# First loads on two DMA queues, folds and K behind the first V tiles, and store waits spread over the queue

## The chip, the cores and the metric

The kernel runs on one core of a Trainium2 chip. A core has a matrix engine (PE, TensorE), three engines for elementwise work (DVE, VectorE; ACT, ScalarE; POOL, GpSimd), a queue engine (SP, SyncE), and 16 DMA engines that move data between the chip's memory and the core's own memory. SP and ACT can both issue DMAs, each on a queue of its own. The metric is device time in microseconds. The median before is 277.26 us over 4 runs (277.1 to 277.8).

## The reference

The kernel computes one transformer block in bf16 on 2048 tokens of width 640: a linear attention with 32 heads of width 20 and a gated MLP with 1536 columns, both fed by the same layer norm, in parallel, plus the input.

```python
def _A_ref(x, wqkv, w_phi, wo):
    qkv = (x @ wqkv).reshape(B, S, 3, H, Dh)           # to q, k, v per head
    pq = einsum("bhsd,hdf->bhsf", q, w_phi)
    pk = einsum("bhsd,hdf->bhsf", k, w_phi)
    phi_q = concatenate([softmax(pq), softmax(-pq)])
    phi_k = concatenate([softmax(pk), softmax(-pk)])
    kv = einsum("bhsf,bhsd->bhfd", phi_k, v)
    z  = einsum("bhsf->bhf", phi_k)
    num = einsum("bhqf,bhfd->bhqd", phi_q, kv)
    den = einsum("bhqf,bhf->bhq", phi_q, z)[..., None] + 1e-6
    return (num / den).reshape(B, S, D) @ wo

def _B_ref(x, w1, w3, w2):
    return (silu(x @ w1) * (x @ w3)) @ w2

xn = _layernorm(x)
return x + _A_ref(xn, ...) + _B_ref(xn, ...)
```

## The kernel before

The 2048 tokens are 16 tiles of 128 (T), or 4 blocks of 512 (NB). The width 640 is 5 chunks of 128 (DC), the MLP's 1536 columns are 12 chunks (FC). The names of the work on PE, in the order in which it first appears:

- **cT** (xc_transpose, L726): the first four tiles of x, with their mean taken off but not yet scaled, are transposed on PE. centre (L719) takes off the mean: ACT sums the tile (an activation with an accumulator, from which z = -mean comes), and DVE or ACT adds z.
- **V** (v_first, L744, for tiles 0 to 3; v_tile, L829, for the others): 10 matmuls of 320 columns against wv. v_first uses the transposes of the centred tile and scales by 1/std when the result leaves PSUM, so it need not wait for the normalised tile.
- **xT** (xn_transpose, L758): the normalised tiles 0 to 3 are transposed on PE into xnT. Tiles 4 to 15 are transposed by DMA (turn, L628).
- **fold** (L783): wk (later wq) is multiplied by w_phi, so that the feature map's first matmul disappears. It needs wqkT, the transposed weights, which five DMA transposes bring (load_wT, L652), and BDc, a block diagonal form of w_phi which POOL builds (block_diag, L774). The result is copied to Wkp.
- **K** (k_tile, L838): 10 matmuls of 320 columns against Wkp, then two Exps on ACT. k_norm (L846) sums on DVE and divides on POOL.
- **MLP columns** (mlp, L955): 10 matmuls of 512 columns, a tanh on ACT, two products on DVE. One column covers 128 of the 1536 and one block of tokens, 512, so the first block's columns need xnT of tiles 0 to 3.
- later: kv_sum, kv_back, q_proj, q_tok (attention's second half) and out_tile (L973), which multiplies by w2 and wo, adds x and stores.

ln_stats (L697) computes mean and variance on DVE and 1/std on POOL; ln_apply (L712) normalises a tile, on DVE for tiles 0 to 3, on DVE or ACT for the later ones.

The order of the instructions is not written by hand. Each operation is recorded with a level (its priority, partly a due time through when) and the engines that could do it, each with a duration. schedule (L168) then plays the kernel in a model: at each step it takes the earliest operation, and between operations that are about equally early the one with the highest level. Constants of the model are MODE (the switch of PE between tile shapes), BACKLOG (how far DMA issues may run ahead of the modelled bus) and the bytes per second of the bus (330e3 bytes per us in commit). The early attribute keeps an operation from being planned before a given time, and filler puts matmuls on zeros into PE's early gaps. The program is fixed when it is built: emit (L384) writes the list of each engine, with a semaphore wait where an operation needs another engine's result, and every engine works through its own list in order. At the end of SP's list stands a wait for every store of the output (L434).

All DMAs are issued by SP. In the order of its list: x tiles 0, 1 and 2; wv in five pieces of one chunk; x tile 3; w_phi; the first 256 columns of w1 and of w3; the five transposes of wk; x tiles 4 to 7; and then the rest of w1 and w3 with x tiles 8 to 11 and 12 to 15 between them; the transposes of xnT as tiles become ready, with those of wq between them.

A single helper records each kind of instruction, so matmuls carry L559, elementwise work L567, plain DMAs L626 and DMA transposes L632; the names of the tiles tell them apart.

Of the kernel before, what the change touches and what calls it, by code (L numbers as in the profile page):

```python
# [2 lines left out]

ACT = mybir.ActivationFunctionType
ALU = mybir.AluOpType
# [4 lines left out]
D = 640  # L10
# [9 lines left out]

ENGINES = ("PE", "ACT", "DVE", "POOL", "SP")
SEM = {"PE": 0.06, "ACT": 0.04, "DVE": 0.04, "POOL": 0.08, "SP": 0.05}
MODE = 0.097
GRAN = 8
BACKLOG = 2.5


def heads_of_chunk(c):
# [37 lines left out]
class _Program:  # L66
# [98 lines left out]

    def schedule(self, start, filler=None, filler_until=0.0):  # L168
        for n, o in enumerate(self.all):
            o.idx = n  # L170
            o.war -= o.raw
# [42 lines left out]
        def commit(o, e, t):  # L214
            nonlocal bus, pool_prev
            o.eng = e
            o.emit, o.busy, dur = o.ways[e]
            o.start = t
            free[e] = t + o.busy
            if o.nbytes:  # L220
                bus = max(bus, t + 0.6) + o.nbytes / 330e3
                o.end = bus + 1.2 + o.extra
            else:
                o.end = t + dur
            o.done = True
# [66 lines left out]
        while left:  # L292
            best = None
            pick = None
            if ready_u:
                t0 = free["PE"]
                blocked = set()
                cands = []
                for u in ready_u:
                    extra = MODE if u.mode != mode else 0.0  # L300
                    u.at = max(unit_time(u), t0 + extra)
                for u in sorted(ready_u, key=lambda u: (-u.level, u.mms[0].idx)):
                    opts = []
                    for k in range(0, 8, u.banks):
                        if blocked & set(range(k, k + u.banks)):
                            continue
                        g = group_time(u, k)
                        if g < 1e8:
                            opts.append((max(g, u.at), fit(k, u.banks, u.at), k))
                    if opts:  # L310
                        x = min(opts)
                        if pick is None or x[0] < pick[0] - (0.03 + MODE):
                            pick = (x[0], u, x[2])
                    if u.banks == 4 and u.at <= t0 + 1.0 and not blocked and (not opts or x[0] > u.at + 0.03):
                        k = min((group_time(u, k, True), k) for k in (0, 4))[1]
                        blocked |= set(range(k, k + 4))
                if pick is not None:
                    best = (pick[0], "PE", pick[1], pick[2])
            moved = False
            for e in ("ACT", "DVE", "POOL", "SP"):  # L320
                if not ready[e]:
                    continue
                ts = [(max(free[e], op_time(o, e)), o) for o in ready[e]]
                t = min(x[0] for x in ts)
                t, o = min((x for x in ts if x[0] <= t + 0.09), key=lambda x: (-x[1].level, x[1].idx))
                if len(o.ways) > 1 and o.level > 1.5e6:
                    other = min(max(free[f], op_time(o, f)) + o.ways[f][2] for f in o.ways if f != e)
                    if other < t + o.ways[e][2] - 0.02:
                        ready[e].remove(o)
                        del o.ways[e]  # L330
                        moved = True
                        continue
                if best is None or t < best[0]:
                    best = (t, e, o, None)
# [49 lines left out]
    def emit(self, finish):  # L384
        nc = self.nc
        for n, o in enumerate(self.ops):
            o.idx = n
        for o in self.ops:
# [22 lines left out]
        for o in self.ops:  # L411
            k = know[o.eng]
            for d in sorted(o.deps, key=lambda d: -d.idx):
# [4 lines left out]
                for a, b in d.clock.items():  # L418
                    if k.get(a, 0) < b:
                        k[a] = b  # L420
                k[key[0]] = max(k.get(key[0], 0), key[1])
            if o.nbytes:
                ndma += 1
                s = nc.alloc_semaphore(f"d{ndma}")
# [6 lines left out]
            else:  # L431
                lists[o.eng].append(("op", o.emit, None, 0))
            o.clock = dict(k)
        for o in finish:  # L434
            lists["SP"].append(("wait", o.sem[2], o.sem[1]))
        return lists
TRIPLES = ((0, 3, 0, 60), (3, 3, 60, 60), (6, 3, 120, 60), (9, 3, 180, 60), (12, 3, 240, 60), (13, 3, 300, 20))


def bass_parallel_sum__linear_kernel_hedgehog__glu_gated_swiglu__prompt_kernel(  # L440
# [134 lines left out]
    def sb(*aps):  # L575
        return [a for a in aps if hasattr(a, "ap")]
# [42 lines left out]

    queue = {"SP": nc.sync, "ACT": nc.scalar}  # L620

    def load(o, i, level=0.0, eng="SP", after=()):
        n = mybir.dt.size(o.dtype)
        for s in o.shape:
            n *= s
        return P.dma(eng, lambda: queue[eng].dma_start(o, i), sb(o), sb(i), n, 0.45, level, after)  # L626

    def turn(o, i, level=0.0, dram=False):  # L628
        n = 2
        for s in o.shape:  # L630
            n *= s
        d = P.dma("SP", lambda: nc.sync.dma_start_transpose(o, i), sb(o), sb(i), n, 1.3 * n / 163840, level)  # L632
        d.extra = 1.0 if dram else 0.2
        return d

# [9 lines left out]
    def load_x(a, b, level, eng="SP"):  # L645
        load(x_tok[:, a:b, :], x_t[:, a:b, :], level, eng)

    def load_w13(a, b, level):
        load(w1_s[:, :, a:b], w1_t[:, :, a:b], level)
        load(w3_s[:, :, a:b], w3_t[:, :, a:b], level)  # L650

    def load_wT(which, e, level):  # L652
        turn(wqkT[:, which * DC + e:which * DC + e + 1, :],
# [6 lines left out]
    def consts():  # L660
        memset("DVE", zero[:], 0.0, 9)
        zeroed.append(P.all[-1])
        memset("DVE", warm[:], 0.0, 9)
        add([w_act(warm[:], warm[:], ACT.Exp, 8)], [warm[:]], [warm[:]], None, 1e9)
# [47 lines left out]
    def ln_apply(t, level):  # L712
        o, m, s, z = x_tok[:, t, :], mv[:, t, 0:1], mv[:, t, 4:5], mv[:, t, 6:7]
        ways = [w_op("DVE", "tensor_scalar", (o, o, m, s, ALU.subtract, ALU.mult), 0.35, 0.44)]
        if t >= 4:
            ways.append(w_act(o, o, ACT.Identity, D, s, z))
        add(ways, [o], [o, m, s, z] if t >= 4 else [o, m, s], None, level)

    def centre(t, level):  # L719
        o, i, z = xc[:, t, :], x_tok[:, t, :], mv[:, t, 6:7]  # L720
        add([way("ACT", "activation", (junk[:], i, ACT.Copy), dict(scale=-1.0 / D, accum_out=z), 0.8, 0.9)],
            [junk[:], z], [i], None, level)
        add([w_op("DVE", "tensor_scalar", (o, i, z, None, ALU.add), 0.35, 0.44), w_act(o, i, ACT.Identity, D, 1.0, z)],
            [o], [i, z], None, level)

    def xc_transpose(t, level):  # L726
        n = 2 if t == 0 else 1
# [287 lines left out]
    lv = 9e5  # L1015
    load_x(0, 1, lv)
    load_x(1, 2, lv - 1)
    load_x(2, 3, lv - 2)
    for c in range(DC):
        load(wv[:, c, :], wqkv_t[:, c, 2 * D:3 * D], lv - 3 - c)  # L1020
    load_x(3, 4, lv - 8)
    load(phi_s[:], phi_t, lv - 9)
    load_w13(0, 256, lv - 10)
    for e in range(DC):
        load_wT(1, e, lv - 12 - e)
    load_x(4, 8, lv - 19)
    load_w13(256, 512, lv - 20)
    load_x(8, 12, lv - 21)
    load_w13(512, 1024, lv - 22)
# [10 lines left out]
    block_diag(0)  # L1040
    late(n, 8.0)
    for t in range(4):
        centre(t, up - t)
        ln_apply(t, 1e5 - t)
    for t in range(4):
        xc_transpose(t, 6e4 - 10 * t + 15)
    for t in range(4):
        xn_transpose(t, 3e4 - t)
    for t in range(4, T, 2):
        ln_stats(t, 2, 1e5 - t)  # L1050
        ln_apply(t, 2e5 - t)
# [5 lines left out]
        return 1000.0 - us  # L1057

    for t in range(4):
        v_first(t, 6e4 - 10 * t)  # L1060
    for dc in range(DC):
        fold(1, dc, 4e4 - dc)
    for t in range(T):
# [29 lines left out]
    for t in range(T):  # L1093
        out_tile(t, when(200 + 5 * t))

    P.schedule({"PE": 1.25, "ACT": 2.1, "DVE": 0.93, "POOL": 0.8, "SP": 0.81}, filler, 12.0)

    lists = P.emit(finish)

# [58 lines left out]
```

## Time and profile before

| | us |
|---|---|
| median of 4 runs | 277.26 |
| the profiled execution | 277.1 |
| its span (first to last instruction) | 275.3 |
| PE busy | 269.3 |
| DVE, ACT, POOL busy | 183.3, 102.0, 60.6 |

A profile shows one execution. For each engine it gives the time in which instructions ran, and the idle time before an instruction with what ended it. The chain that ended last goes back from the last instruction: at each step to what released it, or to the instruction before it on its engine. A DMA's issue is an instruction on the queue; the transfer itself takes longer and ends with a landing. "SPq" is SP's queue, "PEld" the loading of weights into PE, which overlaps with matmuls. Matmuls are pipelined: one of 320 columns is shown with 299 ns, but ten of them start within 1.36 us.

### The profile page before, as it was taken

To read this page: it belongs to the slowest core of one execution; us is meant where nothing else is said; L and a number is where in the kernel's file an instruction comes from. 1 tells how busy PE (TensorE), PEld (TensorE's weight loads), DVE (VectorE), ACT (ScalarE), POOL (GpSimd) and SP (SyncE) were. 2 spreads that over 40 slices of the span, in tenths; PEclk is the share of its full clock that TensorE was granted. 3 is DMA by queue.
4 is the path that set the end of the run, shared out by engine and by line. 5 is a ranking of instruction groups with operands and counts; after the bars stand their busy time and mean duration, and the time that the engine had idled before them with its cause. 6 is when DMAs were issued, how large, how long until landed. Compare 5 with 4: busy or idle time off the path is not lost.

```text
span 275.3 us, 5058 instructions
## 1 busy us (share of the span) xinstructions
PE 269.3 (98%) x2094; PEld 159.1 (58%) x2094; DVE 183.3 (67%) x324; ACT 102.0 (37%) x188; POOL 60.6 (22%) x101
## 2 busy tenths in 40 slices
PE   8999899999999999999999999999999999999996
PEld 4656576656654447544444445677777774444774
DVE  5769789999987443578978979577761215666112
ACT  6555768455454441246673472010000002322000
POOL 3601664999799100000000000000000000000000
PEclk9999999999999999999999999999999999999999
DMA  6989996840000000801211141243342222000001
GB/s 190 212 232 353 282 147 120 140 147 2 0 0 2 0 0 2 280 9 26 48 26 24 27 47 24 74 100 95 97 97 71 74 71 71 2 0 0 26 24 48
DMA packets 41303, 21.98 MB, mean 80 GB/s; under 512 B 27072, under 2 KB 41280, under 8 KB 41280
## 3 DMA queue, kind: packets, MB, share of 16 engines
q1 hardware_dynamic: 41280, 21.66, 31.8%
q8 instruction: 16, 0.26, 0.4%
q14 instruction: 7, 0.06, 0.1%
HBM read 12.81 MB, written 2.62 MB: 56 GB/s over the span
## 4 chain that ended last, share of the span: by engine, by line
PE 84%; SPq 5%; DMA 4%; DVE 3%; ACT 2%; issue 1%; POOL 0%
PE PS L559 84%; SPq L632 3%; DMA xnT<-x_tok 2%; SPq L626 2%; DMA x_tok<-in_A_x_dram 2%; ACT EqT L567 2%; DVE bst L567 1%; POOL mv L567 0%; DVE hT L567 0%; DVE t L567 0%; DVE Wkp L567 0%; DVE den_s L567 0%; DVE xres L567 0%; DVE x_tok L567 0%; DVE mv L567 0%
## 5 line engine op out<-in xcount | busy, mean ns | idle before, releaser
L559 PE MATMUL PS<-xnT,w_s 128*128 128x512 bf16 x480 | 108.6, 379 | 0.9 <-DVE xnT L567 0.6
L559 PEld LDWEIGHTS PS<-xnT,w_s 128*128 128x128 bf16 x480 | 46.1, 98 | 54.5 <-DVE hT L567 0.8
L559 PE MATMUL PS<-w_s,hT 128*128 128x320 bf16 x384 | 55.0, 299 | 0.0
L567 ACT ACTIVATE th<-PS 128x512 f32<-128x512 f32 x48 | 28.8, 599 | 65.1 <-PE PS L559 65.1
L567 DVE SCALAR_TENSOR_TENSOR t<-th,PS 128x512 bf16<-128x512 f32 x48 | 32.9, 684 | 25.4 <-ACT th L567 25.4
L559 PEld LDWEIGHTS PS<-w_s,hT 128*128 128x128 bf16 x384 | 37.1, 98 | 14.9
L567 DVE TENSOR_TENSOR xres<-PS,xres 128x640 bf16<-128x640 f32 (+1 forms) x17 | 13.3, 785 | 41.2 <-PE PS L559 41.2
L567 POOL TENSOR_TENSOR ekt<-ekt,rS 128x640 bf16<-128x640 bf16 x32 | 39.5, 1270 | 4.5 <-DVE rS L567 4.4
L567 DVE SCALAR_TENSOR_TENSOR hT<-t,PS 128x512 bf16<-128x512 bf16 x48 | 32.4, 676 | 1.4 <-PE PS L559 0.3
L567 ACT ACTIVATE EqT<-PS 128x512 bf16<-128x512 f32 x40 | 21.9, 595 | 12.6 <-PE PS L559 12.6
L567 ACT ACTIVATE ekt<-PS 128x640 bf16<-128x640 f32 x32 | 20.8, 701 | 10.4 <-PE PS L559 10.2
L559 PE MATMUL PS<-wo_s,oT 128*128 128x320 bf16 x160 | 24.5, 299 | 0.0
L567 DVE TENSOR_TENSOR prod<-PS,g_s 128x1280 bf16<-128x1280 f32 x16 | 23.8, 1490 | 0.5
L567 DVE TENSOR_REDUCE S<-ekt 128x64 f32<-128x1280 bf16 x16 | 22.9, 1458 | 1.6 <-ACT ekt L567 1.6
L559 PE MATMUL PS<-Wkp,xnT 128*128 128x320 bf16 x160 | 23.9, 299 | 0.0
L559 PE MATMUL PS<-xnT,Wqp 128*128 128x512 bf16 x100 | 23.6, 380 | 0.0
L567 ACT ACTIVATE e_s<-PS 128x64 f32<-128x64 f32 x32 | 9.1, 283 | 37.6 <-PE PS L559 37.1
L559 PE MATMUL PS<-wv,xnT 128*128 128x320 bf16 x120 | 18.3, 299 | 1.0 <-DMA xnT<-x_tok 1.0
L559 PEld LDWEIGHTS PS<-wo_s,oT 128*128 128x128 bf16 x160 | 15.7, 98 | 6.1
L559 PEld LDWEIGHTS PS<-Wkp,xnT 128*128 128x128 bf16 x160 | 15.6, 98 | 6.1
L559 PEld LDWEIGHTS PS<-wv,xnT 128*128 128x128 bf16 x120 | 11.7, 98 | 7.0 <-issue 1.4
L559 PEld LDWEIGHTS PS<-xnT,Wqp 128*128 128x128 bf16 x100 | 9.3, 98 | 10.8
(69 smaller groups left out, 170.8 us busy)
## 6 DMA issues: line engine op xcount, KB each, us to landing
w_s<-in_B_w_dram SPq DMA_DIRECT2D x4, 640.0 KB, 9.0
xres<-in_A_x_dram SPq DMA_DIRECT2D x16, 160.0 KB, 2.3
out_dram<-xres SPq DMA_DIRECT2D x15, 160.0 KB, 1.8
x_tok<-in_A_x_dram SPq DMA_DIRECT2D x3, 640.0 KB, 8.1
w_s<-in_B_w_dram SPq DMA_DIRECT2D x1, 1920.0 KB, 9.1
w_s<-in_B_w_dram SPq DMA_DIRECT2D x4, 320.0 KB, 5.7
wv<-in_A_wqkv_dram SPq DMA_DIRECT2D x5, 160.0 KB, 4.0
wo_s<-in_A_wo_dram SPq DMA_DIRECT2D x1, 800.0 KB, 5.7
```

What stands on the lines that cost most here:

```text
L559: return nc.tensor.matmul(o(u.k), l, r, start=start, stop=stop, skip_group_check=shared)
L567: return getattr(e, name)(*[at(a, u) for a in args], **{k: at(v, u) for k, v in kw.items()})
L626: return P.dma(eng, lambda: queue[eng].dma_start(o, i), sb(o), sb(i), n, 0.45, level, after)
L632: d = P.dma("SP", lambda: nc.sync.dma_start_transpose(o, i), sb(o), sb(i), n, 1.3 * n / 163840, level)
```

## The change

It has these parts.

1. **The first loads.** SP issues x tiles 0 and 1, chunks 0 and 1 of wv as one piece, x tiles 2 and 3, then the five wk transposes, and only then w1 and w3. ACT issues chunks 2 to 4 of wv as one piece and w_phi, directly behind the activation that warms up its table, and later, behind the evacuation of the first V tile, x tiles 4 to 7.
2. **Centring.** The constant CENTRED says which engine centres which of the first four tiles. Tiles 0 and 1 keep the sum on ACT; for tiles 2 and 3 DVE subtracts the mean of the statistics.
3. **Normalising on POOL.** ln_apply of tiles 0 and 1 runs on POOL instead of DVE.
4. **The order on PE.** With the new levels, durations and constants the planner arrives at this: V0 and V1 one behind the other; cT2, xT0, xT1, cT3; V2 and V3; xT2 and xT3; all five folds; K of tiles 0 to 3; five MLP columns; then V4, K4 and so on up to K9 before the next column. Before, it was: V0, cT2, V1, cT3, V2, V3; all four xT; a column; three folds; a column; two folds; a column; K of tiles 0 to 3; a column; then V4 up to K8.
5. **Planner.** The bus is modelled in time per descriptor size instead of bytes; MODE goes from 0.097 to 0.085 and BACKLOG from 2.5 to 5.0; within the first 25 us of the model the planner's tolerances are drawn at random from a fixed seed.
6. **Store waits.** Before the n-th output store SP waits for store n - 4, and at its end only for the last four.

The further order, up to the last instruction, differs in a few places: the wq transposes stand at other places between the xnT transposes, POOL's last divisions change places with two memsets, and one MLP column changes places with two projections of q in the attention's second half.

```diff
-MODE = 0.097
+MODE = 0.085
-BACKLOG = 2.5
+BACKLOG = 5.0
...
+        rng = random.Random(seed)
...
-                bus = max(bus, t + 0.6) + o.nbytes / 330e3
+                bus = max(bus, t + 0.6) + o.nbytes / 1e3
...
+                slack = 0.12 if seed is None or t0 > shaken else rng.choice((0.03, 0.12, 0.12, 0.3, 0.6))
...
-                        if pick is None or x[0] < pick[0] - (0.03 + MODE):
+                        if pick is None or x[0] < pick[0] - slack:
...
+            if o in place and place[o] >= 4:
+                d = finish[place[o] - 4]
+                lists[o.eng].append(("wait", d.sem[2], d.sem[1]))
...
-        for o in finish:
+        for o in finish[-4:]:
             lists["SP"].append(("wait", o.sem[2], o.sem[1]))
...
+CENTRED = {0: "ACT", 1: "ACT", 2: "DVE", 3: "DVE"}
+POOLED = (0, 1)
+SEED = 0
...
+    def bus(o, elem):
+        n = 1
         for s in o.shape:
             n *= s
+        return n * 2 / elem / 16 * max(18.0, 10 + 0.0352 * elem) + 100.0
...
+        if t in POOLED:
+            ways = [w_op("POOL", "tensor_scalar", (o, o, m, s, ALU.subtract, ALU.mult), 1.25, 1.3)]
...
+    def centre(t, level, by):
+        if by == "ACT":
...
+        else:
+            m = mv[:, t, 0:1]
+            add([w_op("DVE", "tensor_scalar", (o, i, m, None, ALU.subtract), 0.35, 0.44)], [o], [i, m], None, level)
...
     load_x(1, 2, lv - 1)
-    load_x(2, 3, lv - 2)
-    for c in range(DC):
-        load(wv[:, c, :], wqkv_t[:, c, 2 * D:3 * D], lv - 3 - c)
-    load_x(3, 4, lv - 8)
-    load(phi_s[:], phi_t, lv - 9)
-    load_w13(0, 256, lv - 10)
+
+    def load_wv(a, b, level, eng):
+        load(wv[:, a:b, :], wqkv_t[:, a:b, 2 * D:3 * D], level, eng)
+    load_wv(0, 2, lv - 2, "SP")
+    load_x(2, 3, lv - 3)
+    load_wv(2, 5, 2e9, "ACT")
+    load_x(3, 4, lv - 4)
+    load(phi_s[:], phi_t, 2e9 - 1e3, "ACT")
     for e in range(DC):
-        load_wT(1, e, lv - 12 - e)
-    load_x(4, 8, lv - 19)
+        load_wT(1, e, lv - 9 - e)
+    load_w13(0, 256, lv - 16)
+    n = len(P.all)
+    load_x(4, 8, 1.9e6, "ACT")
+    late(n, 9.0)
...
     for t in range(4):
-        xc_transpose(t, 6e4 - 10 * t + 15)
-    for t in range(4):
-        xn_transpose(t, 3e4 - t)
+        if t in CENTRED:
+            xc_transpose(t, 6e4 - 10 * t + 15)
+        xn_transpose(t, 3e4 - t if t in CENTRED else 6e4 - 10 * t + 15)
...
-    P.schedule({"PE": 1.25, "ACT": 2.1, "DVE": 0.93, "POOL": 0.8, "SP": 0.81}, filler, 12.0)
+    P.schedule({"PE": 1.25, "ACT": 2.1, "DVE": 0.93, "POOL": 0.8, "SP": 0.81}, filler, 12.0, SEED, 25.0)
```

More of the change, by code (lines that the diff above doesn't have):

```diff
@@ L2 @@
 from concourse import mybir
+import random
 ACT = mybir.ActivationFunctionType
@@ L164, in dma, with schedule @@
         return self.add(o, writes, reads, level, after)
-    def schedule(self, start, filler=None, filler_until=0.0):
+    def schedule(self, start, filler=None, filler_until=0.0, seed=None, shaken=0.0):
+        rng = random.Random(seed)
         for n, o in enumerate(self.all):
@@ L324, in schedule @@
                 t = min(x[0] for x in ts)
-                t, o = min((x for x in ts if x[0] <= t + 0.09), key=lambda x: (-x[1].level, x[1].idx))
+                w = 0.09 if seed is None or t > shaken else rng.choice((0.03, 0.09, 0.09, 0.2, 0.4))
+                t, o = min((x for x in ts if x[0] <= t + w), key=lambda x: (-x[1].level, x[1].idx))
                 if len(o.ways) > 1 and o.level > 1.5e6:
@@ L387, in emit @@
             o.idx = n
+        finish = sorted(finish, key=lambda o: o.idx)
+        place = {o: n for n, o in enumerate(finish)}
         for o in self.ops:
@@ L620, in bass_parallel_sum__linear_kernel_hedgehog__glu_gated_swiglu__prompt_kernel, with load @@
     queue = {"SP": nc.sync, "ACT": nc.scalar}
-    def load(o, i, level=0.0, eng="SP", after=()):
-        n = mybir.dt.size(o.dtype)
+    def bus(o, elem):
+        n = 1
         for s in o.shape:
             n *= s
-        return P.dma(eng, lambda: queue[eng].dma_start(o, i), sb(o), sb(i), n, 0.45, level, after)
+        return n * 2 / elem / 16 * max(18.0, 10 + 0.0352 * elem) + 100.0
+    def load(o, i, level=0.0, eng="SP", after=()):
+        return P.dma(eng, lambda: queue[eng].dma_start(o, i), sb(o), sb(i), bus(o, 2 * o.shape[-1]), 0.45, level,
+                     after)
     def turn(o, i, level=0.0, dram=False):
[L629 to L632, printed above, removed]
+        d = P.dma("SP", lambda: nc.sync.dma_start_transpose(o, i), sb(o), sb(i), bus(o, 256),
+                  1.31, level)
         d.extra = 1.0 if dram else 0.2
@@ L646, in load_x, with load_w13 @@
         load(x_tok[:, a:b, :], x_t[:, a:b, :], level, eng)
-    def load_w13(a, b, level):
-        load(w1_s[:, :, a:b], w1_t[:, :, a:b], level)
-        load(w3_s[:, :, a:b], w3_t[:, :, a:b], level)
+    def load_w13(a, b, level, eng="SP"):
+        load(w1_s[:, :, a:b], w1_t[:, :, a:b], level, eng)
+        load(w3_s[:, :, a:b], w3_t[:, :, a:b], level, eng)
     def load_wT(which, e, level):
@@ L663, in consts @@
         memset("DVE", warm[:], 0.0, 9)
-        add([w_act(warm[:], warm[:], ACT.Exp, 8)], [warm[:]], [warm[:]], None, 1e9)
+        add([w_act(warm[:], warm[:], ACT.Exp, 8)], [warm[:]], [warm[:]], None, 3e9)
         memset("POOL", ident[:], 0.0)
@@ L717, in ln_apply @@
         add(ways, [o], [o, m, s, z] if t >= 4 else [o, m, s], None, level)
-    def centre(t, level):
+    def centre(t, level, by):
         o, i, z = xc[:, t, :], x_tok[:, t, :], mv[:, t, 6:7]
[L721 to L724, printed above, removed]
+        if by == "ACT":
+            add([way("ACT", "activation", (junk[:], i, ACT.Copy), dict(scale=-1.0 / D, accum_out=z), 0.86, 0.92)],
+                [junk[:], z], [i], None, level)
+            add([w_op("DVE", "tensor_scalar", (o, i, z, None, ALU.add), 0.35, 0.44),
+                 w_act(o, i, ACT.Identity, D, 1.0, z)], [o], [i, z], None, level)
+        else:
+            m = mv[:, t, 0:1]
+            add([w_op("DVE", "tensor_scalar", (o, i, m, None, ALU.subtract), 0.35, 0.44)], [o], [i, m], None, level)
     def xc_transpose(t, level):
@@ L1042, in bass_parallel_sum__linear_kernel_hedgehog__glu_gated_swiglu__prompt_kernel @@
     for t in range(4):
-        centre(t, up - t)
+        if t in CENTRED:
+            centre(t, up - t, CENTRED[t])
         ln_apply(t, 1e5 - t)
     for t in range(4):
-        xc_transpose(t, 6e4 - 10 * t + 15)
-    for t in range(4):
-        xn_transpose(t, 3e4 - t)
+        if t in CENTRED:
+            xc_transpose(t, 6e4 - 10 * t + 15)
+        xn_transpose(t, 3e4 - t if t in CENTRED else 6e4 - 10 * t + 15)
     for t in range(4, T, 2):
@@ L1059, in bass_parallel_sum__linear_kernel_hedgehog__glu_gated_swiglu__prompt_kernel @@
     for t in range(4):
-        v_first(t, 6e4 - 10 * t)
+        (v_first if t in CENTRED else v_tile)(t, 6e4 - 10 * t)
     for dc in range(DC):
```

## The prediction

> **What bounds the kernel now.** I read the page's busy shares and the chain that ended last first, then the chain in order of time, then the timelines of PE and of SP's queue over the first 35 us.
>
> ```profile
> PE 269.3 (98%) x2094; PEld 159.1 (58%) x2094; DVE 183.3 (67%) x324; ACT 102.0 (37%) x188; POOL 60.6 (22%) x101
> ```
> ```profile
> 14.25 5.22 DMA x_tok<-in_A_x_dram
> ...
> 26.08 5.96 DMA xnT<-x_tok
> 32.05 0.14 issue
> 32.18 102.14 PE PS L559 x825
> ...
> 144.53 128.21 PE PS L559 x984
> 272.73 0.02 issue
> 272.76 0.49 DVE xres L567
> ```
>
> PE is busy 98% of the span, and from 32.18 us on the chain is nearly all matmul: 102.14, then a seam of some 10 us, then 128.21. The same multiplications have to be done afterwards, so nothing but empty time on PE can be won. Between 40 and 272 us PE has only 0.3 us of it. The rest is before 32.18 us, where the chain is SP's queue, a load of x, statistics and a DMA transpose. PE's own timeline there (start, length, work, idle before it):
>
> ```profile
> 6.34 2.26 PE L559 MATMUL PS<-wv,xcT 128*128 128x320 bf16 x10
> 8.44 0.44 PE L736 MATMUL PS<-ident,xc 128*128 128x128 bf16 x5
> 8.72 1.52 PE L559 MATMUL PS<-wv,xcT 128*128 128x320 bf16 x10
> ...
> 15.33 2.33 PE L559 MATMUL PS<-xnT,w_s 128*128 128x512 bf16 x10 [0.59 <-DVE xnT L567]
> 17.50 1.11 PE L559 MATMUL PS<-BDc,wqkT 128*128 128x140 bf16 x18
> ...
> 28.90 2.32 PE L559 MATMUL PS<-xnT,w_s 128*128 128x512 bf16 x10
> 32.18 1.52 PE L559 MATMUL PS<-wv,xnT 128*128 128x320 bf16 x10 [0.96 <-DMA xnT<-x_tok]
> ```
>
> "Busy" up to 6.3 us is mostly filler. The prizes are the late start of V0 at 6.34 (it waits for wv, chunk by chunk), 0.59 us before the first MLP column, and 0.96 us before V4, which waits for a DMA transpose. SP's queue explains the last one:
>
> ```profile
> 2.19 2.33 SPq L626 DMA_DIRECT2D wv<-in_A_wqkv_dram  x5
> ...
> 7.03 7.18 SPq L632 DMA_TRANSPOSE wqkT<-in_A_wqkv_dram  x5
> 14.25 0.58 SPq L626 DMA_DIRECT2D x_tok<-in_A_x_dram  x1
> ```
>
> x tiles 4 to 7 are issued only behind five wk transposes (1.27 us each, the first 1.93), at 14.25; they land at 19.48, and everything up to V4 hangs on that.
>
> **Step 1, first loads.** Issues cost 0.43 us each, one per 0.47. Before, x0, x1, x2, wv in five pieces and x3 go one behind another. PE's first five pairs of V0 start at 6.2, 6.8, 7.2, 7.7 and 8.15 us as the pieces land, x3 lands at 8.9. In the change SP has x0, x1, two chunks of wv, x2, x3; ACT has the other three chunks and then phi. ACT issues them behind its table load (0.80 to 2.08) and the warming Exp (to 2.30), so at 2.3 and 2.8.
> Does the second queue bring wv sooner? V0's last matmul needs wv, x0 and x1; what shares the bus with it decides. Before, x0 to x2 and wv are 8 x 164 = 1,311 KB. After, if two queues share equally from 3.2 us, ACT's 492 KB finish when SP has also moved 492 KB (its wv piece and x2), behind 328 KB of x0 and x1: 1,312 KB, the same. The windows of 2:4 and 6:8 us show the DMA engines at a share of 0.91 and 1.03 while moving 266 and 285 GB/s. The Trainium skill's page "DMA: Bandwidth & Descriptors" (Issuing engines are not separate DMA queues) speaks against a gain: all queues end on the same 16 engines, and a second one only saves issue time. The row speaks a little the other way: landings 0.48 us apart match the issue rhythm of 0.475, and between 20 and 25 us the same engines move 349 GB/s. By the rule wv is complete at 8.15 as before; by the row, 1,311 KB from 2.0 us at 330 GB/s plus the 1.25 us that now lie between moving and landing, at 7.2. I take 8.15, because shares of 0.9 to 1.0 are a busy bus; 7.2 is the good end, and 8.9 (ACT's part served last, with x3) the bad end.
> What is late next: x2, which landed by 4.95, now lands with wv's end at about 8.15, x3 at 8.8.
>
> **Step 2, V0 to the last transpose.** V0's last six matmuls after 8.15: 0.8, to 8.97; V1 1.36 (ten starts, 0.136 each), to 10.33. Before, PE had V1 done at 10.24 and the transpose of tile 2 as well, so here the change is behind by 0.4.
> DVE is in order: second half of the statistics of x1, first half of x2 (waits for x2), and only behind it tile 1's aggregate. So from 8.2: 0.44, aggregate 0.2 (8.85), x2 to 9.5, x3 first half 9.95, centring tile 2 10.35 (0.39), x3 second half and aggregate 11.0, centring tile 3 11.4, copy of xcT2 11.9 (0.47). ACT loses two centring passes (2 x 0.92); the two DVE centrings stand where they did.
> POOL now normalises tiles 0 and 1. The trace has no POOL operation of that form; nearest is its 128x640 multiply at 1.27 us (two inputs), the lower end is the 0.22 of the 128x1 form. I take 1.27. Tile 1's rstd starts at 8.9, ends 9.7; tile 2's first half 9.95; the normalising of tile 1 to 11.2; then tile 2's and 3's rstd among five BDc products (4 x 0.42 + 0.58), done about 14.9. Before, BDc was done at 11.5 and waited.
> PE then: cT2 at 10.4, xT0, xT1 to 11.5, cT3 to 11.75, V2 from 12.0 (xcT2's copy), V3 to 14.7, xT2 and xT3 to 15.25. Without DVE's lateness it would be 14.85. So the folds start at 15.25, where the old kernel started its first column at 15.33: the front as such wins 0.1.
>
> **Step 3, folds and K directly, columns after.** Before, columns lay between folds to cover the five Wkp copies (ACT 0.67, DVE 0.82). Now: folds 0.95 + 0.68 = 1.63, to 16.9; ACT copies three (15.75 to 17.75, behind V3's evacuation), DVE two (behind two xnT copies, 16.2 to 17.75). K0 needs its bank and chunk 1 at 17.0, chunks 3 and 4 at 17.8, and reaches those 0.8 us after its start. So K starts at 17.05, a loss of 0.2; bounds 0 and 0.8 (K0 standing for all five copies). wk transposes, issued from 3.15 to 10.2 now, land by about 14 (3.0 to 5.3 us after issue). K takes 5.44 (23.46 to 28.90), eight Exps of 0.67 keep its pace.
> Then five columns instead of four before V4: 5 x 2.165 = 10.8. V4 at 17.05 + 5.44 + 10.8 + 0.1 = 33.4.
>
> **Step 4, does V4 still wait?** ACT issues x4 to x7 behind V0's evacuation, at about 10.0 instead of 14.25; its issue was 0.58, and V1's evacuation is queued behind it, with slack. It lands at about 15.2. DVE reaches those statistics after the Wkp copies, at 17.8, normalises at 22. SP issues the transposes at about 22.5 behind all but one of the w1/w3 loads; 5.2 MB left at 10.2 us and 340 GB/s are moved at 25.7, so they land at 27 to 29. V4 at 33.4 has 4 us of cover; without it, 0.96 again. The weights of columns 1 to 4 land by 17, those of the fifth by 24 and it starts at 31. After V4, tiles 8 and 9 come behind one more wq transpose (1.3 us); they are needed at 44. No stall.
>
> **Step 5, store waits.** Before, 17 waits stand at SP's end. But the queue's waits show that it still stood there for the last store:
>
> ```profile
> SPq L1103 <- DMA out_dram<-xres: 0.8, 1, 0.8
> ```
>
> The 13 waits removed are hidden by that 0.8; without it they cost some 0.5 us. Each added one waits for the store four back, landed long ago (1.8 us each, 5 us apart): zero to 0.05, on the last store. Behind them stand only that store and a residual load with slack. New planner constants and seed change only orders; late ones swap a column and two q projections at 155 to 167 us, same work: 0, bounds -0.3 to +0.3 from the seam's own 0.3.
>
> **Sum.** Old V4 with a fifth column ahead: 32.18 + 2.16 = 34.34. New: 33.4. Gain 0.95. The profiled execution took 277.1 with a span of 275.3 and 1.8 around it: it becomes 274.35 and 276.15. The median lies 0.16 above that: **276.3**.
>
> **Rivals.** *Main line* (gain 0.5 to 1.6, 275.7 to 276.7): chance 0.50.
> *The second queue speeds the bus* (for: 349 GB/s later; against: the share already at 0.9): wv at 7.2 and x2 early move folds from 15.25 to some 14.3: 275.3 (275.0 to 275.7). Chance 0.15.
> *The change doesn't do what it says*: wv at 8.9 puts the folds 0.5 to 0.7 later, or the copies stall K by 0.8: 276.7 to 277.8. For: two queues, x3 and transposes compete with wv. Against: equal sharing. Chance 0.17.
> *Slower: PE's clock stays low.* The page's clock row says 9 throughout, but five transposes take 0.74 us at 5.81 and 0.44 at 8.44, and the first V0 matmul 474 ns against 299. So PE reached full speed near 6.9 us, after 5.6 us without a break. The Trainium skill's page "TensorE: Matmul & The Clock Gate" (What's actually happening) says that the clock is raised after a window of some 3.4 us of sustained work. In the change PE idles from 6.3 to 7.1 and again before 8.15. By the row alone the switch comes at 6.9 as before; by the rule a window that covers the idle may fail. Then V0's last six and V1's ten matmuls take 0.267 instead of 0.136: +2.1, 278.4. It decides from the eighth slow matmul on (0.95 / 0.131). Against: the window before 6.3 is as full as now. With it, 0.18.
>
> **Range and chances.** 275.0 (the quick bus) to 278.4 (the slow clock); the likeliest case alone 275.7 to 276.7. A measurement here tells 0.2%, 0.55 us. Faster: 0.50 + 0.15 + 0.02 = 0.67; within: 0.12 of the third case; slower: 0.18 + 0.03 = 0.21.
>
> **What would show it.** wv's last chunk at 8.15 and V0 ending at 9.0; folds starting at 15.25 with BDc done before; K with no gap above 0.3; V4 at about 33.4 with no DMA ahead of it; the tail's wait longer than 0.8. It is wrong if V0 ends after 9.8, if matmuls of 474 ns go on beyond 8 us, if V4 or V5 waits for a transpose, or if PE's idle time moves behind 40 us.

## The result, and the profile after

The median after the change is 276.61 us (276.3 to 277.04, 41 runs); beside it the kernel before took 277.13 us (276.49 to 277.98, 61 runs). The ratio is 0.9979, 95% interval [0.9974, 0.9984]: a gain of 0.58 us by the ratio (0.52 between the medians), where 0.95 was forecast. The profiled span went from 275.3 to 274.9 us.

The busy shares of the kernel after are nearly those of before; POOL alone has 5 us more:

```profile
PE 269.0 (98%) x2097; PEld 159.7 (58%) x2097; DVE 183.0 (67%) x319; ACT 102.6 (37%) x187; POOL 65.6 (24%) x103
```

The chain that ended last, in order of time (start, length, what):

```profile
4.89 0.78 POOL mv L580
5.67 0.10 issue
5.77 2.53 POOL x_tok L580
8.30 0.22 POOL mv L580
8.52 0.07 issue
8.59 0.79 POOL mv L580 x2
9.38 0.01 issue
9.39 2.54 POOL x_tok L580
11.93 0.05 issue
11.98 0.45 PE PS L787 x5
...
15.99 117.77 PE PS L572 x935
```

Before, the chain was SP's queue, a load of x, its statistics and a DMA transpose as far as 32.18 us, and only from there PE. Now PE carries it from 11.98 us on (but for a seam of some 10 us in the middle that both kernels have), and what stands ahead of that is POOL: two normalisings (x_tok, L580) of 2.53 us each, with the 1/std of tile 1 (mv) between them. The prediction had 1.27 us for each of these.

PE's timeline (start, length, work, idle before it) shows the same place from the other side:

```profile
6.92 2.88 PE L572 MATMUL PS<-wv,xcT 128*128 128x320 bf16 x20
...
9.91 0.44 PE L787 MATMUL PS<-ident,x_tok 128*128 128x128 bf16 x5
...
11.98 0.45 PE L787 MATMUL PS<-ident,x_tok 128*128 128x128 bf16 x5 [1.63 <-POOL x_tok L580]
...
12.55 2.88 PE L572 MATMUL PS<-wv,xcT 128*128 128x320 bf16 x20
15.27 0.72 PE L787 MATMUL PS<-ident,x_tok 128*128 128x128 bf16 x10
15.83 1.76 PE L572 MATMUL PS<-BDc,wqkT 128*128 128x140 bf16 x30
17.54 5.61 PE L572 MATMUL PS<-Wkp,xnT 128*128 128x320 bf16 x40
22.98 10.96 PE L572 MATMUL PS<-xnT,w_s 128*128 128x512 bf16 x50
33.77 1.52 PE L572 MATMUL PS<-wv,xnT 128*128 128x320 bf16 x10
```

V0 and V1 now run without a break from 6.92 to 9.63 us, the second of two sets of xT waits 1.63 us for POOL, and from 12 us to V4 nothing waits: V4 starts at 33.77 with no DMA ahead of it. The old kernel with a fifth column before V4 would stand at 34.34, so the front has won 0.57 us. The last DVE operation starts at 272.27 instead of 272.76, 0.49 earlier: the gain is made before V4, and the rest of the kernel passes it on.

Up to the folds the change is still behind: they start at 15.83, where the old kernel's first column stood at 15.33, 0.50 earlier. The gain is V4's wait of 0.96, which is gone, less these 0.50, and 0.11 that is made up between the folds and V4.

ACT's queue, and SP's, show the loads (start, length of the issue, transfer):

```profile
1.26 0.45 ACTq L642 DMA_DIRECT2D wv<-in_A_wqkv_dram  x1
1.74 0.51 ACTq L642 DMA_DIRECT2D phi_s<-in_A_w_phi_dram  x1
...
8.48 0.38 ACTq L642 DMA_DIRECT2D x_tok<-in_A_x_dram  x1
```
```profile
3.30 6.96 SPq L646 DMA_TRANSPOSE wqkT<-in_A_wqkv_dram  x5
...
22.48 7.91 SPq L646 DMA_TRANSPOSE xnT<-x_tok  x4
```

ACT issues wv at 1.26 us, within its table load (0.81 to 2.09) and ahead of the warming Exp that stands before it in ACT's list (2.10); the prediction had 2.3.

### The profile page after: what moved, and what is told of

Read it like the earlier page. It is cut to its first block, busy times and chain, and to the rows that moved or that the text cites. A ratio compares the mean times of both kernels' runs of the same rounds, so it can differ in the third digit from the quotient of the medians.

```text
span 274.9 us, 5072 instructions
## 1 busy us (share of the span) xinstructions
PE 269.0 (98%) x2097; PEld 159.7 (58%) x2097; DVE 183.0 (67%) x319; ACT 102.6 (37%) x187; POOL 65.6 (24%) x103
## 4 chain that ended last, share of the span: by engine, by line
PE 92%; POOL 3%; ACT 2%; DVE 1%; DMA 1%; issue 1%
PE PS L572 91%; POOL x_tok L580 2%; ACT EqT L580 2%; DMA x_tok<-in_A_x_dram 1%; POOL mv L580 1%; PE PS L787 0%; DVE bst L580 0%; DVE hT L580 0%; DVE den_s L580 0%; DVE xres L580 0%; ACT e_s L580 0%; DVE xc L580 0%; PE PS L757 0%; DVE t L580 0%; DVE pr_s L580 0%
## 5 line engine op out<-in xcount | busy, mean ns | idle before, releaser
L580 ACT ACTIVATE th<-PS 128x512 f32<-128x512 f32 x48 | 28.8, 599 | 66.1 <-PE PS L572 66.1
L580 DVE SCALAR_TENSOR_TENSOR t<-th,PS 128x512 bf16<-128x512 f32 x48 | 32.6, 678 | 24.0 <-ACT th L580 24.0
L580 DVE TENSOR_TENSOR xres<-PS,xres 128x640 bf16<-128x640 f32 (+1 forms) x17 | 13.3, 785 | 41.2 <-PE PS L572 41.2
L580 POOL TENSOR_TENSOR ekt<-ekt,rS 128x640 bf16<-128x640 bf16 x32 | 39.5, 1264 | 1.6 <-DVE rS L580 1.6
L580 DVE SCALAR_TENSOR_TENSOR hT<-t,PS 128x512 bf16<-128x512 bf16 x48 | 32.5, 677 | 1.3 <-PE PS L572 0.3
L580 ACT ACTIVATE EqT<-PS 128x512 bf16<-128x512 f32 x40 | 21.9, 594 | 12.6 <-PE PS L572 12.6
L580 DVE TENSOR_REDUCE S<-ekt 128x64 f32<-128x1280 bf16 x16 | 22.9, 1459 | 3.4 <-ACT ekt L580 3.4
L580 DVE TENSOR_TENSOR prod<-PS,g_s 128x1280 bf16<-128x1280 f32 x16 | 23.8, 1490 | 0.5
L580 ACT ACTIVATE ekt<-PS 128x640 bf16<-128x640 f32 x32 | 20.8, 701 | 8.6 <-PE PS L572 8.4
L580 ACT ACTIVATE e_s<-PS 128x64 f32<-128x64 f32 x32 | 9.0, 282 | 37.6 <-PE PS L572 37.1
L580 DVE BATCH_NORM_STATS2 bst<-x_tok 128x6 f32<-128x320 bf16 x32 | 14.2, 468 | 3.1 <-DMA x_tok<-in_A_x_dram 3.1
L572 PEld LDWEIGHTS PS<-xnT,Wqp 128*128 128x128 bf16 x100 | 9.3, 98 | 10.8
```

Of the source, the lines that this page charges most:

```text
L572: return nc.tensor.matmul(o(u.k), l, r, start=start, stop=stop, skip_group_check=shared)
L580: return getattr(e, name)(*[at(a, u) for a in args], **{k: at(v, u) for k, v in kw.items()})
```

## The experiments

Three questions were open: what POOL's normalising costs and why; what of the earlier wv is due to the second queue; and which of the other parts (early x tiles 4 to 7, store waits, filler and clock) carry time. All start from the kernel after and keep its planned order on every engine, except where a new plan is named.

**Both tiles normalised on DVE.**

```diff
...
+    for t in (0, 1):
+        a, (e, (f, busy, dur)) = applied[t]
+        a.eng, a.emit = e, f
...
```

`applied` holds each normalising and the same operation for DVE.

> The changed kernel with its order kept, only the normalising of tiles 0 and 1 runs on DVE instead of POOL. Theory A (POOL's two normalisings of 2.53 us each are what ate the front's gain): PE's wait of 1.6 us before the transpose of tile 1 is gone, V2 starts at about 11.4 instead of 12.55, folds at about 14.7 instead of 15.83, time 1.1 us below the changed kernel: about 275.5, ratio to before 0.994. Theory B (DVE is in order and full, so the wait only moves to the centring of tile 3, to BDc or to the copies): V2 not before 12.2, time 276.3 to 276.8, ratio 0.997 to 0.999.

Measured: 275.12 us (274.92 to 275.57) against 277.11 of before, ratio 0.9933 [0.992, 0.9947]. This beats both kernels. Its PE timeline:

```profile
6.67 2.88 PE L572 MATMUL PS<-wv,xcT 128*128 128x320 bf16 x20 [0.41 <-DMA wv<-in_A_wqkv_dram]
...
9.66 0.72 PE L790 MATMUL PS<-ident,x_tok 128*128 128x128 bf16 x10
...
10.86 2.89 PE L572 MATMUL PS<-wv,xcT 128*128 128x320 bf16 x20
...
32.09 1.52 PE L572 MATMUL PS<-wv,xnT 128*128 128x320 bf16 x10
```

The ten transposes of the normalised tiles 0 and 1 stand in one piece, V2 starts at 10.86 instead of 12.55, V4 at 32.09 instead of 33.77. So POOL's part of the change (part 3) costs 1.3 to 1.5 us (by the ratios, by the medians), and without it the change would win 1.9 to 2.0 us. Theory A had a little less, 1.1; in this trace x2 also happens to land 0.27 us earlier than in that of after (7.14 and 7.41), which helps V2 and V4.

**What the form costs on POOL.** A probe in front of POOL's work, with five forms one behind another, three times over, while DVE has nothing to do:

```diff
...
+            for i in range(3):
+                for form in range(5):
+                    g.wait_ge(s, n)
+                    if form == 0:
+                        r = g.tensor_scalar(a, a, p[:, 0:1], p[:, 1:2], ALU.subtract, ALU.mult)
+                    elif form == 1:
+                        r = g.tensor_scalar(a, a, p[:, 0:1], None, ALU.subtract)
+                    elif form == 2:
+                        r = g.tensor_scalar(a, a, 1.0, 1.0, ALU.subtract, ALU.mult)
+                    elif form == 3:
+                        r = g.tensor_tensor(a, a, c, ALU.mult)
+                    else:
+                        r = g.tensor_scalar(a[:, 0:320], a[:, 0:320], p[:, 0:1], p[:, 1:2], ALU.subtract, ALU.mult)
...
```

> The changed kernel, with 15 extra POOL instructions ahead of all its work, in SBUF that nothing else uses yet, three times each: tensor_scalar 128x640 bf16 with two pointer scalars (the form of the normalising), with one pointer scalar, with two immediate scalars, a 128x640 multiply of two tensors, and the first form on 320 columns. The kernel starts some 25 us later, so its time means nothing. DVE is nearly idle there. Theory L (the form itself is slow): first form about 2.5 us as in the changed kernel, half of it on 320 columns. Theory P (DVE's traffic slowed it): first form at or below the 1.27 us of the multiply.

POOL's timeline in the probe, second round, in the order of the forms:

```profile
12.88 2.50 POOL L1165 TENSOR_SCALAR hT<-hT 128x640 bf16<-128x640 bf16 x1
15.48 1.88 POOL L1167 TENSOR_SCALAR hT<-hT 128x640 bf16<-128x640 bf16 x1
17.45 2.35 POOL L1169 TENSOR_SCALAR hT<-hT 128x640 bf16<-128x640 bf16 x1
19.89 1.39 POOL L1171 TENSOR_TENSOR hT<-hT 128x640 bf16<-128x640 bf16 x1
21.39 1.44 POOL L1173 TENSOR_SCALAR hT<-hT 128x320 bf16<-128x320 bf16 x1
```

With DVE idle, the normalising takes 2.50 us, so the 2.53 in the kernel is no contention with DVE. Two operations with immediate numbers take 2.35, so it is not the two per-row operands either; one operation takes 1.88, a product of two tensors 1.39. Half the columns take 1.44: about 0.38 us are fixed (2 x 1.44 - 2.50), the rest grows with the columns. The whole kernel's time is meaningless here, since all its work starts some 30 us late.

**Only tile 1 on DVE.** The difference from the run with both tiles on DVE:

```diff
-    for t in (0, 1):
+    for t in (1,):
```

> After's order of work, with only tile 1 normalised on DVE; tile 0 stays on POOL. Theory A (it is the second POOL operation, on the chain to xT1, that costs; the first is covered except for what it delays tile 1's rstd on POOL, about 0.3 us): 275.2 to 275.5. Rival B (both cost alike, since they stand one behind the other): half of the gain of 1.5 us, 275.9.

Measured: 275.32 us (275.27 to 275.46) against 276.94, ratio 0.9943 [0.9928, 0.9958]; V2 at 11.29, V4 at 32.52. Most of it, 1.0 to 1.3 us, comes back with tile 1 alone. Tile 0's operation on POOL, as long, costs 0.2 to 0.4 (V4 0.43 later than with both tiles on DVE), since it ends at 8.4 and holds up tile 1's 1/std by some 0.5 us. What counts is which of the two is last in the chain, not their sum.

**An honest cost for the planner.** The normalising stays on POOL, and the planner is told its true length; everything is planned anew.

```diff
-            ways = [w_op("POOL", "tensor_scalar", (o, o, m, s, ALU.subtract, ALU.mult), 1.25, 1.3)]
+            ways = [w_op("POOL", "tensor_scalar", (o, o, m, s, ALU.subtract, ALU.mult), 2.5, 2.55)]
```

> After's kernel with one number changed: the planner is told that POOL's normalising costs 2.5 us (busy) and 2.55 (to the end), instead of 1.25 and 1.3, and plans everything anew with the same seed; the normalising stays on POOL. If the late xT1 is a matter of order only, the planner puts other work there and comes to 275.5 or less. If nothing can fill the place (V2 and the folds need DVE's and POOL's chain in any order), 276.3 to 277.0. A new plan also redraws the order at the seam after 145 us, so a span that differs there is read apart from the first 35 us.

Measured: 276.52 us (276.15 to 277.12) against 276.94, ratio 0.9983 [0.9972, 0.9993], as after the change. The new plan puts V2 before all the xT, folds and one column before K, and three columns behind it. V4 then starts at 31.62 with four columns ahead of it; a fifth (2.16) would bring it to 33.78, where after's stands at 33.77. So this planner, with this seed, found no way around POOL. The delay has only moved: the folds start at 15.27 instead of 15.83 but take 2.26 us instead of 1.76, in part because they wait 0.3 us for BDc, which POOL now builds from 13.99 to 15.95, behind both of its normalisings.

**No tile on POOL, planned anew.**

```diff
-POOLED = (0, 1)
+POOLED = ()
```

> After's kernel with one constant changed: no tile is normalised on POOL, and the planner plans everything anew with the same seed. If the time won by normalising on DVE does not hang on after's plan: 274.8 to 275.6, as with after's order kept (275.12 with both tiles on DVE). If after's order was part of it, or the new order at the seam after 145 us costs: 275.8 to 276.8.

Measured: 275.43 us (275.17 to 275.47) against 277.12, ratio 0.9944 [0.9931, 0.9958]. The gain does not hang on after's order: another plan, with the folds before the last transposes, has V4 at 30.45 with four columns, 32.61 with a fifth, half a microsecond behind the kept order.

**One queue again.** SP issues the second wv piece right behind the first, and w_phi behind x3; nothing else moves. This was run on the kernel after and on the one with both tiles on DVE.

```diff
...
+    sp = [o for o in P.ops if o.eng == "SP"]
+    for a, i, ap, src in ((moved[0], 2, wv[:, 2:5, :], wqkv_t[:, 2:5, 2 * D:3 * D]), (moved[1], 4, phi_s[:], phi_t)):
+        P.ops.remove(a)
+        a.eng, a.emit = "SP", lambda ap=ap, src=src: nc.sync.dma_start(ap, src)
+        P.ops.insert(P.ops.index(sp[i]) + 1, a)
...
```

> The changed kernel with its order kept, only the wv piece of three chunks and w_phi are issued by SP (order: x0, x1, wv 0-1, wv 2-4, x2, x3, w_phi, wk transposes) instead of ACT. Theory Q (the second queue made wv land sooner): V0 has gaps again and V1 ends at 10.2 or later instead of 9.64. Theory O (it was that wv goes ahead of x2 and x3, and in larger pieces): V0 starts before 7.2 without gaps and V1 ends by 9.8. The time can stay at 276.6 either way, because PE waits for POOL until 11.98 in the changed kernel.

> Both edits together: tiles 0 and 1 normalised on DVE, and all first loads on SP. Without POOL's wait the arrival of wv, x2 and x3 should reach the end: theory Q: 0.5 us above the version that only moves the normalising (about 276.0 if that is 275.5). Theory O: the same as that version within 0.2 us.

Measured: on the kernel after 277.12 us (276.57 to 278.43), ratio 1.0013 [0.9996, 1.003]: by the median the whole gain is gone. Four of these twelve executions, at 278.2 to 278.4 us, have a granted clock of 0.994, which none of the 41 of after has; the other eight have a median of 277.0, 0.4 above after. On the kernel with DVE 275.56 us (274.75 to 277.24), ratio 0.9957 [0.9942, 0.9973], 0.44 above its own two-queue form. The first was expected unchanged and is a miss; for the second, theory O had at most 0.2 and theory Q 0.5. Yet it is not wv that holds PE up in the end. In the first kernel's trace:

```profile
6.67 3.19 PE L572 MATMUL PS<-wv,xcT 128*128 128x320 bf16 x20
...
12.41 0.45 PE L787 MATMUL PS<-ident,x_tok 128*128 128x128 bf16 x5 [1.85 <-POOL x_tok L580]
```

V0 starts even earlier than after the change, waits 0.3 us for the second piece of wv, and V1 ends at about 9.8 instead of 9.64. But x2 is issued 0.51 us later and lands at 7.92 instead of 7.41. (Part of that may be chance: x2 lands at 7.14 to 7.57 in the eight traces with two queues, and at 7.41 in the other one with one.) DVE stands at x2's statistics in its list, with tile 1's aggregate behind them, so tile 1's normalising moves by 0.44 us, and PE with it. SP's queue shows the same push:

```profile
2.20 0.47 SPq L1130 DMA_DIRECT2D wv<-in_A_wqkv_dram  x1
2.71 0.96 SPq L642 DMA_DIRECT2D x_tok<-in_A_x_dram  x2
3.71 0.43 SPq L1130 DMA_DIRECT2D phi_s<-in_A_w_phi_dram  x1
4.19 7.87 SPq L646 DMA_TRANSPOSE wqkT<-in_A_wqkv_dram  x5
```

Two issues stand ahead of the wk transposes, which start at 4.19 instead of 3.30. With both tiles on DVE this too reaches PE: V2 starts 0.28 us later (11.14 instead of 10.86), then the folds wait for a transpose, and K starts 0.68 later (16.54 instead of 15.86):

```profile
14.42 0.42 PE L572 MATMUL PS<-BDc,wqkT 128*128 128x140 bf16 x5
15.08 1.50 PE L572 MATMUL PS<-BDc,wqkT 128*128 128x140 bf16 x25 [0.24 <-DMA wqkT<-in_A_wqkv_dram]
```

The second queue thus saved issue time, as the Trainium skill's page "DMA: Bandwidth & Descriptors" (Issuing engines are not separate DMA queues) has it; the page calls that time small, and here 0.9 us of it on SP was worth 0.4 to 0.5 us of the kernel (275.56 - 275.12; 277.12 - 276.61, or 277.0 - 276.61 without the four), because what stands behind it on SP feeds the chain. That wv arrives early is for the larger part not the second queue's work. It is complete at 8.15 before the change, at about 7.5 and 6.9 in the two traces with one queue (issue and time to landing added up), and at about 6.8 and 6.5 in the same kernels with two. On one queue it now comes ahead of x2 and in two pieces instead of five, and its last piece is issued at 2.20 instead of 4.09.

**x tiles 4 to 7 back on SP,** behind the wk transposes and four weight loads.

```diff
...
+    sp = [o for o in P.ops if o.eng == "SP"]
+    P.ops.remove(moved)
+    moved.eng, moved.emit = "SP", lambda: nc.sync.dma_start(x_tok[:, 4:8, :], x_t[:, 4:8, :])
+    P.ops.insert(P.ops.index(sp[13]) + 1, moved)
...
```

`moved` is the load of x tiles 4 to 7.

> After's order of work, but tiles 4 to 7 of x are issued by SP at about 13.9 us, behind the wk transposes and four weight loads (near where the kernel before issued them, at 14.25), instead of by ACT at 8.48. Theory C (the fifth column ahead of V4 is the cover): x lands at 19 to 20, its transposes are issued at about 26 and land near 32, V4 at 33.8 as in after: same time as after, 276.6, at most 0.3 more. Rival E (the early issue is what removed V4's wait): V4 waits 0.9 to 1 us for the transpose, 277.5.

Measured: 276.85 us (276.56 to 277.48) against 277.12, ratio 0.999 [0.9978, 1.0001]. SP's queue and PE:

```profile
13.16 0.90 SPq L1128 DMA_DIRECT2D x_tok<-in_A_x_dram  x1
...
24.21 6.11 SPq L646 DMA_TRANSPOSE xnT<-x_tok  x4
```
```profile
33.66 0.30 PE L572 MATMUL PS<-wv,xnT 128*128 128x320 bf16 x1
34.11 1.40 PE L572 MATMUL PS<-wv,xnT 128*128 128x320 bf16 x9 [0.15 <-DVE hT L580]
```

The load is issued nearly where it was before the change, 4.7 us later than after it, and V4 has no DMA ahead of it; a break behind its first matmul, in part for a DVE product, costs some 0.3. So the 0.96 us which V4 waited before were removed by the fifth column and the work that now stands ahead of V4, not by the early issue. Even the landing of the kernel before, at 32.05, would be in time for 33.66.

**Store waits back at the end.**

```diff
-            if o in place and place[o] >= 4:
-                d = finish[place[o] - 4]
-                lists[o.eng].append(("wait", d.sem[2], d.sem[1]))
...
-        for o in finish[-4:]:
+        for o in finish:
```

> After's kernel with the 17 waits for the stores back at the end of SP's list, as before the change; nothing else moves. Theory H (the waits were hidden by the wait for the last store): the same time as after within 0.1 us, 276.6 (0.9979 of before), and the wait for the last store 0.2 to 0.4 us shorter than the 1.2 us of after, because SP comes to it later. Rival S (each wait at the end costs time): 13 waits of about 35 ns come on top, 277.0 to 277.1, which would be nearly the whole of the change's measured gain.

Measured: 276.61 us (276.45 to 278.62) against 276.94, the median of after to the hundredth. The ratio, 0.9996 [0.9981, 1.001], has a wide interval that overlaps with after's and does not decide by itself; one of the eleven executions, 278.62 us at a granted clock of 0.994, widens it. The trace does: the span is 274.8 against 274.9, the last DVE operation starts at 272.24 against 272.27, and from there to the end of the span it is 2.6 us in both; only the wait for the last store differs. First this kernel's queue waits, then those of after (total, times, longest):

```profile
SPq L1127 <- DMA out_dram<-xres: 0.8, 1, 0.8
```
```profile
SPq L1130 <- DMA out_dram<-xres: 1.2, 1, 1.2
```

SP comes to the last store's wait 0.4 us earlier when the others are spread, and then waits 0.4 longer.

**The clock, without filler.** The kernel with both tiles on DVE, without the matmuls on zeros that fill PE before V0.

```diff
...
+    P.ops = [o for o in P.ops if o in P.all]
...
```

> The kernel with tiles 0 and 1 normalised on DVE, without the matmuls of zeros that fill PE before V0; every other instruction in its order. Rule of the clock (the clock rises only after some microseconds of sustained work): V0 starts at 6.7 as before but its matmuls, and V1's, take 0.267 us each instead of 0.136 until about 3 us of work have passed, so V1 ends 1.3 to 2.6 us later and the span is 274.3 to 275.8 instead of 273.2. If the clock does not depend on the work before: 0.136 us each from the start, span 273.2.

Measured: one run, 276.1 us, span 274.4 against 273.2 with the filler. PE's timeline:

```profile
4.53 0.72 PE L760 MATMUL PS<-ident,xc 128*128 128x128 bf16 x5 [4.53 <-DVE xc L580]
5.54 0.71 PE L760 MATMUL PS<-ident,xc 128*128 128x128 bf16 x5 [0.30 <-DVE xc L580]
6.68 4.44 PE L572 MATMUL PS<-wv,xcT 128*128 128x320 bf16 x20 [0.42 <-DMA wv<-in_A_wqkv_dram]
...
12.07 2.88 PE L572 MATMUL PS<-wv,xcT 128*128 128x320 bf16 x20
```

V0 starts at the same time, but V0 and V1 take 4.44 us instead of 2.88: (4.44 - 2.88) / 0.131 = 12 of the 20 matmuls ran slow, until about 9.9 us, 3.2 us after V0 began and 5.4 after PE's first transposes began. The Trainium skill's page "TensorE: Matmul & The Clock Gate" (What's actually happening) has the clock rise after a window of some 3.4 us of sustained work, which runs freely and does not start with the kernel. The row agrees with a wait of a few microseconds of work; the length of a window no run here shows. V2, and with it V4 (33.30 against 32.09), is 1.2 us later.

The probe of POOL, in which PE idles from 4.75 to 33.73 us, shows the same a second time, and there the page's clock row (tenths of full speed in slices of 7.6 us) shows it too:

```profile
PEclk9555599999999999999999999999999999999999
```

In that trace V0 and V1 take 4.71 us from 35.82 on, and the granted clock is 0.50 until 39 us and 1.00 from 40 on, more than 5 us after PE's first work. So the clock rival of the prediction is a real mechanism with a real price (one run each); here the filler holds it off.

## Why the prediction was right, and where its numbers were not

The direction, the place and most of the chain were right; the gain came out 0.4 us smaller. That it came so near is luck: x2 came 0.75 us earlier than the sum had it, tile 1's normalising with what held it up took 1.5 us longer, and the two errors largely cancelled. With POOL's term alone wrong, the step's own sum has the transposes of tile 1 at 12.46 (11.2 + 1.26) instead of 11.98, and V4 near 34.25 against the 34.34 of before (an estimate): almost no gain.

- **Step 1, first loads: mis-sized.** Forecast: wv complete at 8.15, V0 ending at 8.97, V1 at 10.33. Measured: no wait for wv from 6.92 on, V1 ending at about 9.64, so 0.7 us were won. Three things failed. ACT issued at 1.26, not behind its table load and the Exp at 2.3. And equal sharing of a full bus was too careful: between 4 and 6 us the DMA engines moved 357 GB/s at a share of 1.11, before only 223 at 0.86, so a share of 0.9 was no full bus. And issue time was left out: the five pieces landed 3.1 to 4.1 us after issues that went on until 4.09, the two pieces, issued at 1.26 and 1.73, landed 4.3 and 5.1 us after. The rule about queues was not wrong, as the one-queue runs show: the place ahead of x2 and the larger pieces bring wv earlier on one queue too. x2 landed at 7.41, not 8.15, and DVE's chain moved forward with it.
- **Step 2, V0 to the last transpose: the term that failed.** Normalising on POOL was sized by the 128x640 product (1.27 us) because it was the nearest row. It takes 2.53. By the step's own sum, 11.2 + 1.26 for tile 1's operation - 0.75 for the early x2 gives 11.7; tile 0's long operation holds up tile 1's 1/std (0.26 from 8.01 to 8.27), which makes 11.97. Measured: the transposes of tile 1 begin at 11.98. V2 came at 12.55 (12.0 forecast) and the folds at 15.83 (15.25).
- **Step 3, folds and K: right.** The folds took 1.71 us until K, with 0.1 of stall (1.63 and 0.2 forecast); K's 5.44 and the columns' 10.8 stand in the timeline. BDc was ready at 15.29, before the folds, as said. V4 came at 33.77, 0.37 later than forecast: 0.58 from step 2, less 0.2 that this step had allowed for stalls.
- **Step 4, V4: the outcome right, the reason too rich.** V4 has no DMA ahead of it and nothing waits for a transpose after it. The early issue by ACT was listed as the cause; with the load back on SP it is nearly as good (0.24 us more in the medians, with overlapping ranges).
- **Step 5, store waits and seam: right.** The waits cost nothing, and the tail's wait grew from 0.8 to 1.2 as forecast.
- **The rivals.** The quick bus did come in its effect (V0 as early as its case had it), but its time of 275.3 did not, since POOL took it back; with DVE in POOL's place the kernel runs in 275.12. "The change doesn't do what it says" is close in time, 0.1 us away, for another reason: wv was early and the copies did not stall K; POOL did the harm. The slow clock did not occur in the kernel after: its 41 executions have a granted clock of 0.999 or more. It is not far off, though: 4 of 12 executions with one queue and 1 of 11 with the store waits back have 0.994 and take 1.2 to 2.0 us more than the others of their kernel. By the 0.50 that the probe shows, 0.006 of 277 us is some 3.3 us at half the clock (an estimate). No trace of such an execution was kept, so where these microseconds lie is not shown.

What stays open: how the earlier wv divides between its place in the order and its larger pieces; what the new order on PE, with a fifth column ahead of V4, would win in the kernel before with its old loads, since V4's wait accounts for more than the whole gain; and what centring on DVE and the planner's new constants are worth. None of these was tried alone.

## What to carry to other kernels

A helper engine's operation is sized by its own form, not by a neighbour of the same shape: the two-step tensor_scalar took about twice as long on POOL as a product with two inputs, and 5.7 times DVE's 0.44 us. When work is moved to an idle engine, look for the operation that is last before the bound engine; that one costs most (tile 1's 1.0 to 1.3 us of the 1.5), and it is the one to leave on the fast engine. And a gain in front of such a chain shows only when each wait in the row behind it is gone: the second queue's 0.4 to 0.5 us were real because they fed the same chain, while the early load of x was not needed.

## What the runs showed of the hardware that was not expected

- POOL's tensor_scalar on 128x640 bf16 takes 2.50 us with two per-row operands, 2.35 with two immediates, 1.88 with one operation; a product of two such tensors 1.39 in the same probe, 1.26 in the kernel.
- ACT's queue issues DMAs while the table load runs (1.26 and 1.74, the load from 0.81 to 2.09), ahead of an activation that stands before them in the list and starts at 2.10. The same at 8.48, where the load of x is issued while the evacuation before it has only just begun (8.47).
- The time at which PE reaches its full speed differs between executions. Five transposes took 0.45 us from 4.53 on in the run with tile 1 on DVE, still 0.74 at 5.81 after the change, though both began their filler at 1.25 or 1.26. The profile's clock row shows full speed in all of them, and in the run without filler too, where a V0 or V1 matmul had a median of 468 ns against 299. In the probe, behind an idle PE, the row does fall to 0.50. So a clock row at full speed in a kernel's first microseconds does not show that PE had it; the durations do.
- One DVE normalising took 1.71 us in the kernel after (13.78), where the same form takes 0.44, while POOL's products of BDc ran from 13.71 to 15.29. In the run with tile 1 on DVE two of the same operations took 0.94 together beside the same products. Running side by side is therefore not enough to cause it; what else it takes was not tried. PE only just did not wait for it: it ended at 15.49, and the transposes that read it stand in a row without a gap from 15.27 on.
